# Loading and transposing K in column quarters with interleaved heads, in a one-token decode block

## The chip, the cores and the metric

The kernel runs on one core of one Trainium2 chip. The metric is the device time of one execution in microseconds; the time before is the median of three runs. A profile of one execution stands beside it, with its own span.

## What is computed

One token `x` of 1024 numbers goes through a layer norm, and then through an attention branch and an MLP branch whose results are added to it. Everything in memory is bf16. Cut to what matters:

```python
xn = layernorm(x)                                  # 1 x 1024
q  = xn @ wq                                       # 32 heads of 128
k, v = last 4096 rows of k_cache, v_cache          # 4 kv heads, 4096 x 128 each
o  = softmax(q . k / sqrt(128)) . v                # 8 query heads share one kv head
A  = o @ wo                                        # wo: 4096 x 1024
h  = gelu(layernorm(xn) @ w1 + b1)                 # w1: 1024 x 3584
B  = h @ w2 + b2                                   # w2: 3584 x 1024
out = x + A(xn) + B(xn)
```

In the code the residual `x` and the bias `b2` enter the final accumulator `accf` through a small matmul. K and V of the window are 4 MB each, wq and wo 8 MB each, w1 and w2 7 MB each: 39.85 MB are read once, and almost nothing is written.

## The kernel before, in words

The large operands go through a ring of four slots of 32 KB per partition (4 MB each). The tiles in the order of their requests are `k_sb`, `wq0`, `wq1`, `kt_scr` (a scratch tile that no DMA fills), `w10`, `w11`, `v_sb`, `w20`, `w21`, `wo0`, `wo1`. A tile's load is issued on SP's queue when the slot's last user has finished; SP takes its issues in the order of the program, so a load that waits holds up those behind it. Small loads (`x_sb`, `b1_row`, `xb2`) go on ACT's queue. The framework orders the instructions of each engine and adds the waits; a DMA also waits for the completion counter that it reuses (there are eight, handed out in turn).

**K.** Each of the four heads is loaded by one DMA of 1 MB (line 73). Partition p gets 32 consecutive keys of the head, 8 KB in one run. The scores need K with the head's 128 features on the partitions. That is done in two steps. DVE transposes each head in blocks of 32x32 into `kt_scr` (line 185, four instructions of 128x4096). Then 64 copies of 32x1024 put the blocks in their places in `kT`; they are shared out between ACT (line 199, 26 copies) and DVE (line 201, 38 copies). `kT` holds, for each head, 4096 keys side by side.

**q and the scores.** 64 matmuls (line 237) make q from `xnT` and the two halves of wq. q is copied to `q_sb`, transposed on PE (`qT_ps`, line 261) and spread into `qm` (line 266), which holds for each kv head its 8 query columns and zeros elsewhere. The scores of all 32 heads over a quarter R of the keys are then the sum of four matmuls, one per kv head (line 275), each with 512 keys as the moving operand; the four R write four groups of 32 partitions of the PSUM tile `sp`.

**Softmax and output.** Maximum over the row (lines 283 to 294), exponential on ACT (line 297), a block transpose (`eTb`, line 299), the row sums (`rs_ps`, line 301), and 32 matmuls with V into `o_all` (line 319), of which a mask keeps each head's own kv head (line 322).

**MLP and the end.** `acch` takes 64 matmuls with the halves of w1 (line 257: `w10`, then `w11`), then gelu (line 312) and a transpose to `hT` (line 314). The final product runs over 28+28 chunks of w2 and 16+16 chunks of wo (line 338 into `accf`; the last eight chunks on line 353 into `acct`, in four pieces of 256 columns). `wo1` is loaded in five DMAs that become smaller towards the end (line 228). The result is added up on DVE (line 356) and stored.

Of the kernel before, what the change touches and what calls it, by code (L numbers as in the profile page):

```python
# [9 lines left out]
BF16 = mybir.dt.bfloat16  # L10
# [6 lines left out]
def kernel(  # L17
# [14 lines left out]
    nc = tc.nc  # L32
    P = 128
    D = A_x.shape[-1]
    Hkv = A_k_cache.shape[1]
    Sk = A_k_cache.shape[2]
# [5 lines left out]
    W = min(4096, max(256, Sk // 4))  # L42
    C = D // P
    NCH = W // P
    NJQ = NQ // 512
    WQ4 = W // 4
# [7 lines left out]

    consts = ctx.enter_context(tc.tile_pool(name="consts", bufs=1))
    small = ctx.enter_context(tc.tile_pool(name="small", bufs=2))
    ring = ctx.enter_context(tc.tile_pool(name="ring", bufs=4))
    ps_acc = ctx.enter_context(tc.tile_pool(name="ps_acc", bufs=1, space=bass.MemoryType.PSUM))
    ps_tp = ctx.enter_context(tc.tile_pool(name="ps_tp", bufs=1, space=bass.MemoryType.PSUM))
    ps_f = ctx.enter_context(tc.tile_pool(name="ps_f", bufs=2, space=bass.MemoryType.PSUM))  # L60

    RING_ELEMS = 16384

    def ring_tile(name):
        return ring.tile([P, RING_ELEMS], BF16, tag="ring", name=name, align_bytes=256)

    x_flat = A_x.rearrange("a b d -> (a b d)")


    k_sb = ring_tile("k_sb")  # L70
    k4 = k_sb[:].rearrange("p (g c d) -> p g c d", g=Hkv, c=NCH)
    for g in range(Hkv):
        nc.sync.dma_start(out=k4[:, g, :, :], in_=A_k_cache[0, g, Sk - W:Sk, :].rearrange("(p c) d -> p c d", p=P))
    x_sb = consts.tile([P, C], BF16)
    nc.scalar.dma_start(out=x_sb[:], in_=x_flat.rearrange("(p c) -> p c", p=P))
    xb2 = consts.tile([34, 512], BF16)
# [10 lines left out]
    for i in range(2):  # L87
        t = ring_tile(f"wq{i}")
        tv = t[:].rearrange("p (r n) -> p r n", r=4)
        nc.sync.dma_start(out=tv, in_=wq_v[:, 4 * i:4 * i + 4, :])  # L90
        wq_tiles.append(tv)
    kt_scr = ring_tile("kt_scr")


# [13 lines left out]
    qm = consts.tile([P, Hkv, Hq], BF16)  # L108
# [69 lines left out]
                         start=True, stop=False, tile_position=(pr, pr))  # L178


    kT = consts.tile([P, Hkv, W], BF16)
    scr = kt_scr[:].rearrange("p (g f) -> p g f", g=Hkv)
    k2 = k_sb[:].rearrange("p (g f) -> p g f", g=Hkv)
    for g in range(Hkv):
        nc.vector.transpose(out=scr[:, g, :], in_=k2[:, g, :])  # L185
    nc.vector.tensor_reduce(out=sel4[:], in_=ident_f[:].rearrange("p (r h) -> p h r", r=4), axis=AX.X, op=ALU.add)
    act_share = [11, 8, 5, 2]
    act_moves, dve_moves = [], []
    for g in range(Hkv):
        T4 = scr[:, g, :].rearrange("p (c a j) -> p c a j", a=4, j=32)  # L190
        k = 0
        for R in range(4):
            for Cd in range(4):
                src = T4[32 * R:32 * R + 32, :, Cd, :]
                dst = kT[32 * Cd:32 * Cd + 32, g, WQ4 * R:WQ4 * (R + 1)].rearrange("p (c j) -> p c j", j=32)
                (act_moves if k < act_share[g] else dve_moves).append((dst, src))
                k += 1
    for (dst, src) in act_moves:
        nc.scalar.copy(out=dst, in_=src)  # L199
    for (dst, src) in dve_moves:  # L200
        nc.vector.tensor_copy(out=dst, in_=src)  # L201

    for i in range(2):
        t = ring_tile(f"w1{i}")
# [3 lines left out]
    v_sb = ring_tile("v_sb")  # L208
    v4 = v_sb[:].rearrange("p (g c d) -> p g c d", g=Hkv, c=NCH)
    for g0, g1 in ((0, 2), (2, 3), (3, 4)):  # L210
        src = A_v_cache[0, g0:g1, Sk - W:Sk, :].rearrange("g (p c) d -> p g c d", p=P)
# [20 lines left out]
    for i, w3 in enumerate(wq_tiles):  # L232
        for r in range(4):
            c = 4 * i + r
            for j in range(NJQ):
                b, t = divmod(j, 4)
# [10 lines left out]
    for j in range(8):  # L247
        t, b = divmod(j, 2)
        nc.tensor.matmul(acch[32 * t:32 * t + 1, b, :NH], lhsT=ones_bf[0:1, 0:1], rhs=b1_row[:, j * NH:(j + 1) * NH],
                         start=True, stop=False, tile_position=(0, 32 * t))  # L250
    for i, w3 in enumerate(w1_tiles):
        for r in range(4):
            c = 4 * i + r
            for b in range(2):
                for t in range(4):
                    j = 2 * t + b
# [5 lines left out]
    for g in range(Hkv):  # L262
        b, th = divmod(g, 2)
        src = qT_ps[:, b * 4:(b + 1) * 4, 64 * th:64 * th + 64:32]
        dst = qm[:, g, g * REP:(g + 1) * REP].rearrange("p (t hh) -> p hh t", t=2)
# [4 lines left out]
    for a in range(WQ4 // 512):  # L270
        sp = ps_f.tile([P, 512], FP32, tag="pf", name="sp")
        for R in range(4):
            for g in range(Hkv):
                c0 = WQ4 * R + 512 * a
                nc.tensor.matmul(sp[32 * R:32 * R + 32, :], lhsT=qm[:, g, :], rhs=kT[:, g, c0:c0 + 512],  # L275
                                 start=(g == 0), stop=(g == Hkv - 1), tile_position=(0, 32 * R))
        if a % 2 == 0:
            nc.vector.tensor_copy(out=sc[:, a * 512:(a + 1) * 512], in_=sp[:])
        else:
            nc.scalar.copy(out=sc[:, a * 512:(a + 1) * 512], in_=sp[:])  # L280
# [63 lines left out]
    for t in range(4):  # L344
        half, w = divmod(t, 2)
        src = accf[32 * half:32 * half + 1, 256 * w:256 * w + 256]
# [41 lines left out]
```

## Time and profile before

| what | value |
|---|---|
| median of 3 runs | 102.22 us (102.2 to 102.45) |
| span of the profiled execution | 100.7 us |
| read from memory over the span | 39.86 MB, mean 396 GB/s |
| busy: PE, DVE, ACT, POOL | 49.1, 49.4, 34.2, 4.5 us |
| DVE, block transposes (line 185) | 4 of 4.41 us |
| DVE, kT copies (line 201) | 38 of 0.419 us |
| ACT, kT copies (line 199) | 26 of 1.042 us |
| PE, scores (line 275) | 32 matmuls, 3.8 us together |

The span is what the profiler recorded of one execution; the timed runs lie about 1.5 us above it, and the profiled execution has no time of its own beside its span. Busy time of an engine is a sum over the whole span; the page's second part cuts the span into 40 slices of 2.52 us and gives, for each engine, the busy share of each slice in tenths. The "DMA" row is the mean share of the sixteen DMA engines, and GB/s what they moved. The chain that ended last is followed back from the last instruction, at each step to what released it. The trace also records each DMA packet with its size, start and duration, which the text calls the packet records.

### The profile page before, as it was taken

The page shows a single profiled execution, that of the slowest core. Times are in us where ns is not written, and L with a number is a line of the kernel's source. Part 1 is how long each engine was busy: PE and PEld are TensorE (multiplying, and loading weights), DVE is VectorE, ACT ScalarE, POOL GpSimd, SP SyncE. Part 2 cuts the span into 40 slices and gives each one's busy share as a digit, 9 for nine tenths or more (in the row PEclk, how much of TensorE's full clock was granted, in tenths as well). Part 3 has the DMA queues.
Part 4 walks back from the last instruction along what each step waited for, and adds up shares of the span by engine and source line. Part 5 has one row for each costly group of instructions (what it writes and reads, how often), then busy time and mean ns, then how long its engine had stood idle before and what let it go on. Part 6 is the DMA issues. An engine that isn't in the chain of part 4 may idle for free.

```text
span 100.7 us, 962 instructions
## 1 busy us (share of the span) xinstructions
PE 49.1 (49%) x361; PEld 19.2 (19%) x361; DVE 49.4 (49%) x91; ACT 34.2 (34%) x37; POOL 4.5 (4%) x18
## 2 busy tenths in 40 slices
PE   0027200008500930482882935999389930299830
PEld 0012200003100300121531222334133410023310
DVE  4335499999999999997126115510630000000130
ACT  0500002999999999962001045400000000000110
POOL 7105300000000000000000000000000000000000
PEclk9999999999985579555555555569976997559995
DMA  3899999999999998999999998999999998999910
GB/s 52 346 434 436 482 443 482 443 430 417 417 417 391 456 444 376 459 444 382 391 423 430 436 511 387 467 428 433 433 410 413 456 456 384 423 420 408 369 33 1
DMA packets 3031, 39.92 MB, mean 396 GB/s; under 512 B 458, under 2 KB 466, under 8 KB 851
## 3 DMA queue, kind: packets, MB, share of 16 engines
q1 hardware_dynamic: 2872, 39.85, 93.3%
q8 instruction: 3, 0.05, 0.2%
q10 hardware_dynamic: 154, 0.01, 0.1%
q14 instruction: 2, 0.01, 0.0%
HBM read 39.86 MB, written 0.00 MB: 396 GB/s over the span
## 4 chain that ended last, share of the span: by engine, by line
DVE 37%; DMA 24%; PE 19%; issue 9%; POOL 3%; ACT 2%; SPq 2%; POOLq 1%; DVEq 0%; ACTq 0%
DMA wo<-in_A_wo_dram 24%; DVE kt_scr L185 17%; DVE kT L201 16%; PE o_all L319 10%; PE sp L275 4%; PE acch L257 3%; SPq L228 2%; ACT e L297 1%; DVE eTb L299 1%; DVE m_loc L283 1%; PE qT_ps L261 1%; DVE q_sb L240 1%; POOLq L383 1%; ACT sc L280 1%; POOL spread L113 1%
## 5 line engine op out<-in xcount | busy, mean ns | idle before, releaser
L199 ACT COPY kT<-kt_scr 32x1024 bf16<-32x1024 bf16 x26 | 27.1, 1042 | 12.9 <-DVE kt_scr L185 12.6
L185 DVE STREAM_TRANSPOSE kt_scr<-k_sb 128x4096 bf16<-128x4096 bf16 x4 | 17.4, 4412 | 0.0
L201 DVE COPY kT<-kt_scr 32x1024 bf16<-32x1024 bf16 x38 | 15.9, 419 | 0.5
L237 PE MATMUL accq<-wq,xnT 128*1 128x512 bf16 x64 | 7.1, 622 | 17.9 <-DMA wq<-in_A_wq_dram 17.9
L350 ACT COPY bulk<-accf 1x256 f32<-1x256 f32 x2 | 0.7, 361 | 31.7 <-DVE bulk L348 31.7
L348 DVE COPY bulk<-accf 1x256 f32<-1x256 f32 x2 | 0.8, 416 | 21.3 <-PE accf L338 20.8
L319 PE MATMUL o_all<-v_sb,eTb 128*32 128x512 bf16 x32 | 9.9, 485 | 1.0 <-DVE zcol L310 1.0
L338 PE MATMUL accf<-wo,o 128*1 128x512 bf16 x48 | 7.1, 465 | 6.1 <-DMA wo<-in_A_wo_dram 6.1
L257 PE MATMUL acch<-w,yT 128*1 128x448 bf16 x64 | 6.3, 574 | 5.6 <-DMA w<-in_B_w_dram 5.6
L338 PE MATMUL accf<-w,hT 128*1 128x512 bf16 x56 | 7.9, 452 | 0.0
L237 PEld LDWEIGHTS <-xnT 128*1 128x1 bf16 x64 | 2.1, 115 | 22.1 <-issue 22.1
L319 PEld LDWEIGHTS <-eTb 128*32 128x32 bf16 x32 | 3.7, 119 | 6.8 <-issue 3.8
L338 PEld LDWEIGHTS <-o 128*1 128x1 bf16 x48 | 2.4, 98 | 10.8 <-issue 8.9
L275 PE MATMUL sp<-kT,qm 128*32 128x512 bf16 x32 | 3.8, 629 | 0.3 <-DVE qm L266 0.3
L257 PEld LDWEIGHTS <-yT 128*1 128x1 bf16 x64 | 2.0, 116 | 9.4 <-issue 9.4
L131 PE MATMUL ln_tot<-st,ones_f 128*128 128x1 f32 x2 | 0.6, 362 | 6.4 <-DVE st L129 6.4
L338 PEld LDWEIGHTS <-hT 128*1 128x1 bf16 x56 | 2.7, 96 | 4.7 <-issue 2.3
L322 DVE TENSOR_TENSOR o_m<-o_all,grs 32x512 f32<-32x512 f32 x1 | 0.7, 679 | 5.6 <-PE o_all L319 5.6
L297 ACT ACTIVATE e<-sc,nmx 128x1024 bf16<-128x1024 f32 x1 | 1.1, 1147 | 5.7 <-DVE nmx L294 5.7
L314 DVE STREAM_TRANSPOSE hT<-h_sb 128x896 bf16<-128x896 bf16 x1 | 1.7, 1711 | 2.4 <-ACT h_sb L312 2.4
L261 PE MATMUL qT_ps<-ident,q_sb 128*128 128x128 bf16 x8 | 1.2, 308 | 2.3 <-DVE q_sb L240 2.3
L275 PEld LDWEIGHTS <-qm 128*32 128x32 bf16 x32 | 2.1, 133 | 1.4 <-issue 0.9
(84 smaller groups left out, 34.4 us busy)
## 6 DMA issues: line engine op xcount, KB each, us to landing
w<-in_B_w_dram SPq DMA_DIRECT2D x4, 3584.0 KB, 26.1
wq<-in_A_wq_dram SPq DMA_DIRECT2D x2, 4096.0 KB, 21.6
k_sb<-in_A_k_cache_dram SPq DMA_DIRECT2D x4, 1024.0 KB, 7.1
wo<-in_A_wo_dram SPq DMA_DIRECT2D x1, 4096.0 KB, 29.4
v_sb<-in_A_v_cache_dram SPq DMA_DIRECT2D x1, 2048.0 KB
v_sb<-in_A_v_cache_dram SPq DMA_DIRECT2D x2, 1024.0 KB, 23.4
wo<-in_A_wo_dram SPq DMA_DIRECT2D x1, 2048.0 KB
wo<-in_A_wo_dram SPq DMA_DIRECT2D x1, 1024.0 KB, 23.1
```

The source lines that it names most:

```text
L185: nc.vector.transpose(out=scr[:, g, :], in_=k2[:, g, :])
L199: nc.scalar.copy(out=dst, in_=src)
L201: nc.vector.tensor_copy(out=dst, in_=src)
L228: nc.sync.dma_start(out=tv[:, a:b, :], in_=wo_v[:, nr * i + a:nr * i + b, :])
L237: nc.tensor.matmul(accq[32 * t:32 * t + 1, b, :], lhsT=xnT[:, c:c + 1], rhs=w3[:, r, j * 512:(j + 1) * 512], start=(c == 0), stop=(c == C ...
L257: nc.tensor.matmul(acch[32 * t:32 * t + 1, b, :NH], lhsT=yT[:, c:c + 1], rhs=w3[:, r, j * NH:(j + 1) * NH], start=False, stop=(c == C - 1) ...
L261: nc.tensor.transpose(qT_ps[:, b * 4 + hh, :], q_sb[:, b, hh * Dh:(hh + 1) * Dh], ident[:])
L275: nc.tensor.matmul(sp[32 * R:32 * R + 32, :], lhsT=qm[:, g, :], rhs=kT[:, g, c0:c0 + 512], start=(g == 0), stop=(g == Hkv - 1), tile_posit ...
L297: nc.scalar.activation(out=e128[:], in_=sc[:], func=ACT.Exp, bias=nmx[:], scale=scale, accum_out=l_loc[:])
L314: nc.vector.transpose(out=hT[:], in_=h_sb[:].rearrange("p (d c) -> p c d", c=CW2))
L319: nc.tensor.matmul(o_all[:].rearrange("h g d -> h (g d)"), lhsT=eTb[:, 32 * c:32 * c + 32], rhs=v4[:, :, c, :], start=(c == 0), stop=(c == ...
L338: nc.tensor.matmul(accf[32 * half:32 * half + 1, :], lhsT=vec[kind](c), rhs=wap[:, half * 512:(half + 1) * 512], start=False, stop=(idx == ...
```

## The change

K is loaded by two DMAs instead of four. Partition p = 4r+g now holds head g's 128 consecutive keys from row 128r on, 32 KB in one run; the first DMA brings the first 8 KB of every partition (1 MB), the second the remaining 24 KB (3 MB). The four block transposes work on column quarters s of the tile, 32 keys of each partition, instead of heads, so the first needs the first DMA alone. `kT` is laid out as [R][s][1024], where the heads alternate from column to column. ACT copies six of the sixteen block pairs quarter by quarter (24 copies of 32x1024), DVE the other ten for all quarters at once (10 copies of 32x4096). The score matmuls pick a head's keys out of `kT` with a stride of four elements and write their columns of `sp` in an order with a stride of four, so that `sp` has the keys in the same order as before.

The ring's four slots are now named by hand. In the built program the last users differ in one place: w20 follows `kt_scr` and w21 follows `w10`, where it was the other way round. The built program also changes the order on two engines. On DVE the first block transpose stands in the first layer norm, between `ve` (line 143 before) and `xn_f` (line 146 before); the other three stand behind `yT` as before. On PE the transposes of q and the scores stand ahead of both halves of w1, the first half of w1 follows behind `mT_ps`, and the second half behind `rs_ps`, ahead of `o_all`. SP's first wq load no longer waits for a completion counter.

```diff
-    ring = ctx.enter_context(tc.tile_pool(name="ring", bufs=4))
+    ring = ctx.enter_context(tc.tile_pool(name="ring", bufs=1))
...
+    slots = {"k_sb": 0, "wq0": 1, "wq1": 2, "kt_scr": 3, "w10": 1, "w11": 0, "v_sb": 2, "w20": 3, "w21": 1, "wo0": 0, "wo1": 2}
+
     def ring_tile(name):
-        return ring.tile([P, RING_ELEMS], BF16, tag="ring", name=name, align_bytes=256)
+        return ring.tile([P, RING_ELEMS], BF16, tag=f"ring{slots[name]}", name=name, align_bytes=256)
...
-    k4 = k_sb[:].rearrange("p (g c d) -> p g c d", g=Hkv, c=NCH)
-    for g in range(Hkv):
-        nc.sync.dma_start(out=k4[:, g, :, :], in_=A_k_cache[0, g, Sk - W:Sk, :].rearrange("(p c) d -> p c d", p=P))
+    k_v = A_k_cache[0, :, Sk - W:Sk, :].rearrange("g (r c) d -> r g (c d)", r=P // Hkv)
+    for a, b in ((0, W), (W, 4 * W)):
+        nc.sync.dma_start(out=k_sb[:, a:b], in_=k_v[:, :, a:b])
...
-    kT = consts.tile([P, Hkv, W], BF16)
-    scr = kt_scr[:].rearrange("p (g f) -> p g f", g=Hkv)
-    k2 = k_sb[:].rearrange("p (g f) -> p g f", g=Hkv)
-    for g in range(Hkv):
-        nc.vector.transpose(out=scr[:, g, :], in_=k2[:, g, :])
+    NS = 4
+    kT = consts.tile([P, 4, NS, W // NS], BF16)
+    scr = kt_scr[:].rearrange("p (s f) -> p s f", s=NS)
+    k2 = k_sb[:].rearrange("p (s f) -> p s f", s=NS)
+    for s in range(NS):
+        nc.vector.transpose(out=scr[:, s, :], in_=k2[:, s, :])
...
-    act_share = [11, 8, 5, 2]
-    act_moves, dve_moves = [], []
-    for g in range(Hkv):
-        T4 = scr[:, g, :].rearrange("p (c a j) -> p c a j", a=4, j=32)
...
-    for (dst, src) in act_moves:
-        nc.scalar.copy(out=dst, in_=src)
-    for (dst, src) in dve_moves:
-        nc.vector.tensor_copy(out=dst, in_=src)
+    T5 = kt_scr[:].rearrange("p (s c a j) -> p s c a j", s=NS, a=4, j=32)
+    pairs = [(R, Cd) for R in range(4) for Cd in range(4)]
+    ACT_PAIRS = 6
+    for s in range(NS):
+        for (R, Cd) in pairs[:ACT_PAIRS]:
+            nc.scalar.copy(out=kT[32 * Cd:32 * Cd + 32, R, s, :].rearrange("p (c j) -> p c j", j=32),
+                           in_=T5[32 * R:32 * R + 32, s, :, Cd, :])
+    for (R, Cd) in pairs[ACT_PAIRS:]:
+        nc.vector.tensor_copy(out=kT[32 * Cd:32 * Cd + 32, R, :, :].rearrange("p s (c j) -> p (s c) j", j=32),
+                              in_=kt_scr[32 * R:32 * R + 32, :].rearrange("p (c a j) -> p c a j", a=4, j=32)[:, :, Cd, :])
...
-                c0 = WQ4 * R + 512 * a
-                nc.tensor.matmul(sp[32 * R:32 * R + 32, :], lhsT=qm[:, g, :], rhs=kT[:, g, c0:c0 + 512],
+                kv = kT[:, R, :, :].rearrange("p u (b r h) -> p h b u r", r=8, h=Hkv)[:, g, 16 * a:16 * a + 16]
+                nc.tensor.matmul(sp[32 * R:32 * R + 32, :].rearrange("p (b r u) -> p b u r", r=8, u=4), lhsT=qm[:, g, :], rhs=kv,
                                  start=(g == 0), stop=(g == Hkv - 1), tile_position=(0, 32 * R))
```

More of the change, by code (lines that the diff above doesn't have):

```diff
@@ L178 @@
                          start=True, stop=False, tile_position=(pr, pr))
-    kT = consts.tile([P, Hkv, W], BF16)
-    scr = kt_scr[:].rearrange("p (g f) -> p g f", g=Hkv)
-    k2 = k_sb[:].rearrange("p (g f) -> p g f", g=Hkv)
-    for g in range(Hkv):
-        nc.vector.transpose(out=scr[:, g, :], in_=k2[:, g, :])
-    nc.vector.tensor_reduce(out=sel4[:], in_=ident_f[:].rearrange("p (r h) -> p h r", r=4), axis=AX.X, op=ALU.add)
-    act_share = [11, 8, 5, 2]
-    act_moves, dve_moves = [], []
-    for g in range(Hkv):
-        T4 = scr[:, g, :].rearrange("p (c a j) -> p c a j", a=4, j=32)
[L191 to L197, printed above, removed]
-    for (dst, src) in act_moves:
-        nc.scalar.copy(out=dst, in_=src)
-    for (dst, src) in dve_moves:
-        nc.vector.tensor_copy(out=dst, in_=src)
+    NS = 4
[4 more added lines that the diff above has]
+        nc.vector.transpose(out=scr[:, s, :], in_=k2[:, s, :])
+    nc.vector.tensor_reduce(out=sel4[:], in_=ident_f[:].rearrange("p (r h) -> p h r", r=4), axis=AX.X, op=ALU.add)
+    T5 = kt_scr[:].rearrange("p (s c a j) -> p s c a j", s=NS, a=4, j=32)
[8 more added lines that the diff above has]
+                              in_=kt_scr[32 * R:32 * R + 32, :].rearrange("p (c a j) -> p c a j", a=4, j=32)[:, :, Cd, :])
     for i in range(2):
```

## Prediction

> **What bounds the kernel now.** I read the page's forty slices first, because the shares of whole engines (DVE 49%, PE 49%) say little about a kernel in stages.
>
> ```profile
> span 100.7 us, 962 instructions
> ...
> DVE  4335499999999999997126115510630000000130
> ACT  0500002999999999962001045400000000000110
> ...
> DMA  3899999999999998999999998999999998999910
> ...
> q1 hardware_dynamic: 2872, 39.85, 93.3%
> ```
>
> DVE and ACT are full from about 13 to 47 us: that is the transposing of K, the work this change rewrites. But the DMA row is full from the second slice to the end. The table by stretches sharpens it (columns: us, PE, PEld, DVE, ACT, POOL busy, granted clock, DMA share, GB/s):
>
> ```profile
> 13.00:31.00 18.00, 3.52 (x32) 1.06 (x32) 17.94 (x7) 13.77 (x14) 0.00 (x0) 0.96 1.01 435
> 32.00:50.00 18.00, 9.14 (x84) 3.64 (x87) 15.10 (x39) 12.93 (x13) 0.00 (x0) 0.59 0.99 420
> 61.00:76.00 15.00, 12.47 (x50) 4.78 (x52) 4.78 (x10) 2.44 (x3) 0.00 (x0) 0.73 1.00 431
> 95.00:96.00 1.00, 0.49 (x16) 0.26 (x9) 0.52 (x2) 0.36 (x1) 0.00 (x0) 1.00 0.62 225
> 96.00:97.00 1.00, 0.66 (x12) 0.27 (x12) 0.01 (x1) 0.36 (x1) 0.00 (x0) 1.00 0.11 43
> ```
>
> At a DMA share of 1.0 all sixteen DMA engines are busy; between 3 and 95 us the stream never falls dry. In the last microsecond before 97 a share of 0.11 means 1.8 of 16 engines: a straggler ends the load. Now the chain that ended last (start us, us, what):
>
> ```profile
> 71.39 0.02 issue
> 71.40 0.33 SPq L228
> ...
> 73.20 24.12 DMA wo<-in_A_wo_dram
> 97.32 0.04 issue
> 97.36 0.31 PE acct L353 x4
> ```
>
> The chain runs through the transposes and copies because the last pieces of wo were issued when o_all released the slot of v_sb. It overstates that link. The 24.12 us are no transfer of 256 KB: at 430 GB/s they are 10 MB, w2, wo0 and wo1 queued in front. wo0 ended at 86.4 by the packet records, so the issue at 71.4 came about 15 us before the queue would have run dry. So the kernel is one 39.85 MB stream, from the first packet at 2.1 to the last at 97.3 us, and a tail of 3.4 us.
>
> **Part by part.**
>
> *Two K loads instead of four.* K is 4 MB in 512 packets of 8 KB; it becomes 128 of 8 KB and 128 of 24 KB. The packet records give 309 ns for 8 KB and 1213 for 32 KB, so a packet costs (4x309-1213)/3 = 7.7 ns beyond its bytes. Each engine carries 16 packets fewer: 16x7.7 = 0.12 us less, and two completions fewer at 9 ns each. Sum: -0.14 us, on the path, because the stream is the path.
>
> *Interleaved heads.* Consecutive packets of an engine now lie 16 MB apart instead of 8 KB. The nearest row is the first load of v_sb, whose packets alternate between two heads 16 MB apart: its packets take 309 ns, and v_sb as a whole ran at 424 GB/s. So I take zero. The lower bound is zero too, as 309 ns is already the per-byte pace of 32 KB packets. For the upper end see the first rival.
>
> The Trainium skill (DMA: Bandwidth & Descriptors, Latency and other measured facts) warns that HBM row pitches at large powers of two cut the copy rate to about half from 4 MiB up. If that held for this pattern, the K stage would double, by an estimate from that page; the v_sb row contradicts it here.
>
> *Small loads and issues.* On SP two K issues of about 0.4 us go, and wq no longer waits for x_sb (3.1 us today): its two issues move from 5.95 to about 2. K is still in transfer until 12, so nothing is gained. But x_sb, b1 and xb2 on ACT's queue alternate packet by packet with K. Their last packet started at 7.95; against 0.91 us packets I expect about 12 (seven rounds more at 0.91). x_sb itself lands some 0.7 us later.
>
> *First transpose ahead of the layer norm's end.* It now stands between `ve` and `xn_f` on DVE. Queued behind it for 4.41 us are xn_f, xnT and yT; the PE waits for them. xnT moves from 10.2 to about 15, needed at 22.9, when wq0 lands: covered by 8 us. yT goes to about 17, needed after 41. Start of transposes two to four: 12.6+4.4+0.4 (x_sb) = 17.4; end 17.4+3x4.41 = 30.6, against 30.03 today. w11 waits for that; its slot is needed when w10 has landed, at 41.7. Hidden by 11 us; without that cover it would cost 0.6.
>
> *Copies.* DVE: 38 of 32x1024 at 419 ns (15.9 us) become 10 of 32x4096. Bounds: four times 419 = 1.68 us each, or, taking 150 ns of 419 as fixed (the 157 ns of the 8-element copy L266), 0.16+4x0.26 = 1.20 us. I take the second, since L266 shows the fixed part: 12 us, end at 42.7 (upper bound 47.4; today 46.47). ACT: 24 instead of 26 at 1.04 us, six per quarter, ends at about 41. Nothing of it reaches the stream: w20, which now takes kt_scr's slot first, issues at 43 to 48, and v_sb keeps the queue busy until 60.2.
>
> *Order on PE.* qT and the scores move in front of both halves of w1, and the second half moves behind rs_ps. So the end of `sp` is 42.7+0.7 (q_sb)+1.25 (qT)+0.4 (qm)+3.8 = 48.9. The chain behind it to rs_ps took 7.8 us (52.6 to 60.4); then w11's 3.2 us stand in front of o_all: 59.9. v_sb lands at 60.2 and takes over as the late one. o_all: 9.9 us, until about 70.2 (today 71.4). w21 waits for w10's matmuls, at 54.5; w20 lands near 69. All covered.
>
> *Strided scores.* The 32 matmuls L275 read bf16 at 8-byte steps and write PSUM at 16-byte steps. No row shows a strided matmul. Below: no cost (3.8 us as now; less is excluded, as the columns are the same). Above: no overlap at all between the four column groups, 32x629 ns = 20.1 us, +16.3. Nearest strided row: DVE's reduction L324, 1007 ns for 512 strided elements against 679 for L322, 1.5 times. I take 1.5, +1.9 us, inside the cover of 10 us (second rival).
>
> The Trainium skill (Advanced Engine Details and Errata, PSUM Cachelines) states that any non-contiguous PSUM pattern slows matmuls significantly, without a figure; by it the score stage is where this change loses, by my working it does not matter below 3.6 times.
>
> **The sum**, against the profiled span of 100.7 us: -0.14, giving 100.55. The runs' median of 102.22 lies 1.5 us above the span, outside the recorded program; so 102.1. I forecast 102.05, leaving a little for the straggler.
>
> **The rivals.**
>
> *The K load slows down.* Each engine's share of K is now cut out of a 32-row source with four heads, and onto which partitions each engine writes at one moment is not shown by any row. If engines get in each other's way, the cost is undiluted. Price: a dozen packets of w1 between 34.5 and 38 us were stretched from 1062 to 1127-1305 ns; about 1220, 15%, on K's 9.9 us is +1.5. Two engines sharing one path, 309 to 618 ns, is +9.9, 112. It decides from 3% on (0.3 us). Against it: v_sb's row. For it: that row has 128 rows on both sides. 102.4 to 112; chance 0.14.
>
> *The scores become the bound.* PE must start on wo by 90.3 (97.3 less 5.2 for 48 matmuls at full clock and 1.8 to 2 for the last 32), so o_all must end by about 80: 10 us later than forecast. That is sp at 13.8 us, 3.6 times today's. At the upper bound of 20.1 us the end moves by about 16.3-10 = +6, 108. Chance 0.08.
>
> *The straggler catches up.* Most engines finish at 95.5 to 96, one at 97.3. It lost its time in packets stretched from 1062 to about 1550 ns at 47.1 and 68.8, beside 16 KB instruction fetches, and at the start. If fewer instructions or other small-load times spare it one such hit, the end comes 0.5 to 1.0 us earlier: 101.2 to 101.7. For it: 28 DVE instructions fewer. Against: PE, with most instructions, keeps its 720. Chance 0.18.
>
> *DMA-bound, nothing visible moves*: 102.05, own range 101.75 to 102.4. Chance 0.60.
>
> **How the numbers follow.** This kernel's measurement can tell about 0.3% (0.3 us) from no change, so "same" is 101.9 to 102.5. Of the 0.60, 0.45 fall inside, 0.13 below, since -0.14 is half of the bound, and 0.02 above. The straggler's 0.18 is faster. The two slow rivals give 0.22, of which 0.02 inside the bound. Faster 0.31, same 0.47, slower 0.22. The range leaves out 0.05 below 101.4 and 0.15 above 103.6: it takes in the 15% of the first rival, but not its doubling nor most of the second.
>
> **What would show it.** Right: the DMA row full from the second slice to 95 us, K's second load landed near 12, transposes ending near 31, kT copies 1.2 us each, sp under 10 us, o_all starting when v_sb has landed, the last chain again ending in wo. Wrong: a GB/s row under 400 in slices 2 to 5 (first rival); PE accf on wo no longer waiting for DMA, 6.1 us today (second); the last wo landing before 97.0 with the same bytes (third). A dry stretch anywhere between 13 and 95 us would refute my covers.

## The result, and the profile after

The changed kernel takes 102.73 us (median of 11 runs, 102.45 to 102.92) beside 102.27 for the kernel before (11 runs): ratio 1.0034, 95% interval 1.0019 to 1.0048. By this ratio it is slower by about 0.35 us (0.19 to 0.49; the two medians lie 0.46 apart), where the forecast was 102.05, a gain of 0.17. The sign was wrong. The fewer packets that the forecast built on are there all the same, but a late start of about 0.45 us that it left out outweighs them.

The page of the changed kernel, its first two parts and the third:

```profile
span 100.7 us, 929 instructions
...
DVE  4659779999999997102706320000900000000040
ACT  0500797899999972002044500000000000000020
...
DMA  1899999999999898998999998998999999999910
...
q1 hardware_dynamic: 2584, 39.85, 92.8%
```

DVE is done with K in the sixteenth slice (39 us) instead of the nineteenth, ACT in the fifteenth instead of the eighteenth, and 288 DMA packets are gone. Neither moved the end. In the DMA row the first digit is 1 instead of 3; behind it three slices show an 8 for a 9 and one a 9 for an 8. The span itself can't show the loss: this execution took 102.45 us, the lowest of its eleven, whose spans go from 100.7 to 101.1. So the loss has to be looked for where each execution is alike, at the start. SP's issues (start us, us for all of the group), first of the kernel before, then of the changed one:

```profile
0.80 2.02 SPq L73 DMA_DIRECT2D k_sb<-in_A_k_cache_dram  x4
5.95 0.81 SPq L90 DMA_DIRECT2D wq<-in_A_wq_dram  x2
```

```profile
0.80 1.29 SPq L75 DMA_DIRECT2D k_sb<-in_A_k_cache_dram  x2
2.13 1.43 SPq L92 DMA_DIRECT2D wq<-in_A_wq_dram  x2
```

Four issues took 2.02 us and two take 1.29. Taken singly, the first one went from 378 to 654 ns. Now the first microseconds by stretches (the last two columns are the DMA share and GB/s), before and after:

```profile
1.00:2.00 1.00, 0.00 (x0) 0.00 (x0) 0.79 (x4) 0.00 (x0) 0.95 (x5) 1.00 0.82 98
3.00:4.00 1.00, 0.00 (x0) 0.00 (x0) 0.28 (x1) 1.00 (x1) 0.00 (x0) 1.00 0.99 410
```

```profile
1.00:2.00 1.00, 0.00 (x0) 0.00 (x0) 0.79 (x4) 0.00 (x0) 0.95 (x5) 1.00 0.04 1
3.00:4.00 1.00, 0.41 (x2) 0.41 (x2) 0.51 (x3) 0.88 (x1) 0.00 (x0) 1.00 0.88 352
```

Before, DMA engines were at work on K by 2 us; after, the stretch from 1 to 2 us holds nothing but x_sb's first small packets. By the packet records, set on a clock on which SP's first issue starts at 0.80, K's first packet starts at 1.82 us before and at 2.27 after. (The 2.1 us of the prediction was read with the records 0.3 us late; differences are not touched by that.) From there the K stage is as fast as it was: its 4.19 MB take 11.00 us before (to 12.82) and 10.93 after (to 13.20). So the stream starts 0.45 us late, and the K stage does not make it up.

These two profiles do not show the loss at the end. When w1's first packet starts, the changed kernel is 0.40 us behind (32.10 against 31.70), but the last packet of wo ends at 96.92 against 96.99. Packets were stretched more in the execution before: the durations of its packets of 1 KB and more add up to 0.96 us per engine above the undisturbed ones, against 0.61 after. That a late start reaches the end is shown by the times of the runs, here and below.

The changed kernel's chain ends in wo, as before:

```profile
37.52 23.14 DMA v_sb<-in_A_v_cache_dram
60.66 0.14 issue
60.80 9.68 PE o_all L317 x32
70.48 0.02 issue
...
72.29 24.90 DMA wo<-in_A_wo_dram
97.19 0.04 issue
97.24 0.31 PE acct L351 x4
```

Now the chain goes from load to load; the transposes are no longer in it, and o_all starts when v_sb has landed.

### The profile page after: what moved, and what is told of

Same layout as the page of the kernel before. It is cut to its first block, busy times and chain, and to the rows that moved or that the text cites. A ratio compares the mean times of both kernels' runs of the same rounds, so it can differ in the third digit from the quotient of the medians.

```text
span 100.7 us, 929 instructions
## 1 busy us (share of the span) xinstructions
PE 48.8 (48%) x361; PEld 18.9 (19%) x361; DVE 45.0 (45%) x63; ACT 32.1 (32%) x35; POOL 4.5 (4%) x18
## 4 chain that ended last, share of the span: by engine, by line
DMA 78%; PE 13%; SPq 4%; issue 1%; DVE 0%; DVEq 0%
DMA wq<-in_A_wq_dram 30%; DMA wo<-in_A_wo_dram 25%; DMA v_sb<-in_A_v_cache_dram 23%; PE o_all L317 10%; PE accq L235 4%; SPq L226 2%; SPq L75 1%; SPq L210 1%; SPq L92 1%; DVE res L354 0%; PE acct L351 0%; DVEq L354 0%
## 5 line engine op out<-in xcount | busy, mean ns | idle before, releaser
L195 ACT COPY kT<-kt_scr 32x1024 bf16<-32x1024 bf16 x24 | 25.0, 1043 | 7.4 <-DVE kt_scr L188 7.1
L198 DVE COPY kT<-kt_scr 32x4096 bf16<-32x4096 bf16 x10 | 12.2, 1219 | 0.2
L336 PE MATMUL accf<-wo,o 128*1 128x512 bf16 x48 | 8.2, 522 | 6.5 <-DMA wo<-in_A_wo_dram 6.5
L273 PE MATMUL sp<-kT,qm 128*32 128x512 bf16 x32 | 5.9, 922 | 0.3 <-DVE qm L264 0.3
L255 PE MATMUL acch<-w,yT 128*1 128x448 bf16 x64 | 3.4, 352 | 0.0
L278 ACT COPY sc<-sp 128x512 f32<-128x512 f32 x1 | 0.6, 585 | 6.9 <-PE sp L273 6.9
L276 DVE COPY sc<-sp 128x512 f32<-128x512 f32 x1 | 0.7, 691 | 3.8 <-PE sp L273 3.8
```

The lines of the kernel that those rows point to most:

```text
L195: nc.scalar.copy(out=kT[32 * Cd:32 * Cd + 32, R, s, :].rearrange("p (c j) -> p c j", j=32), in_=T5[32 * R:32 * R + 32, s, :, Cd, :])
L198: nc.vector.tensor_copy(out=kT[32 * Cd:32 * Cd + 32, R, :, :].rearrange("p s (c j) -> p (s c) j", j=32), in_=kt_scr[32 * R:32 * R + 32, :] ...
L255: nc.tensor.matmul(acch[32 * t:32 * t + 1, b, :NH], lhsT=yT[:, c:c + 1], rhs=w3[:, r, j * NH:(j + 1) * NH], start=False, stop=(c == C - 1) ...
L273: nc.tensor.matmul(sp[32 * R:32 * R + 32, :].rearrange("p (b r u) -> p b u r", r=8, u=4), lhsT=qm[:, g, :], rhs=kv, start=(g == 0), stop=( ...
L336: nc.tensor.matmul(accf[32 * half:32 * half + 1, :], lhsT=vec[kind](c), rhs=wap[:, half * 512:(half + 1) * 512], start=False, stop=(idx == ...
```

## The experiments

Theory 1: the end of the kernel is the end of the stream, the stream starts 0.45 us later because the first issue on SP takes longer, and that goes through one for one; 0.14 comes back through fewer packets. Theory 2: the 24 KB packets or the 16 MB steps cost time somewhere later in the stream. Theory 3: the strided scores or the new order on PE reach the end.

**A plain source.** Same cuts, same partitions, same number of DMAs:

```diff
-    k_v = A_k_cache[0, :, Sk - W:Sk, :].rearrange("g (r c) d -> r g (c d)", r=P // Hkv)
+    k_v = A_k_cache[0, 0, Sk - 4 * W:Sk, :].rearrange("(p c) d -> p (c d)", p=P)
```

> The changed kernel with the same two K loads (8 and 24 KB per partition, all 128 partitions), but from one contiguous 4 MB piece of one head, so that the source has two dimensions (128 rows) instead of three (32 rows, 4 heads, a run). It leaves out the right keys: the scores are of other rows. Theory 1 (late start: SP's first K issue takes 654 instead of 378 ns, the first K packet starts at 2.27 instead of 1.82 us, and the whole stream with it): first issue about 0.4 us, first packet about 1.8, time 102.27-0.14, about 102.1 to 102.25, some 0.45 below the changed kernel's 102.73. Theory 2 (the packets of 24 KB or the loss of two DMAs make a later part of the stream slower): first issue as short as before, time stays near 102.7. Theory 3 (strided scores or the new order on PE reach the end): time stays near 102.7.

Measured: 102.34 us beside 102.39, ratio 0.9995 (0.9982 to 1.0007). SP's K issues, and the stretch from 1 to 2 us:

```profile
0.80 0.85 SPq L75 DMA_DIRECT2D k_sb<-in_A_k_cache_dram  x2
```

```profile
1.00:2.00 1.00, 0.00 (x0) 0.00 (x0) 0.79 (x4) 0.00 (x0) 0.95 (x5) 1.00 0.48 74
```

The first issue is back at 378 ns, the first packet at 1.80, and the loss is gone, with the transposes by quarters, the strided scores and PE's new order all in place. This excludes theory 3 and the size of the packets. It removes the late start and the 16 MB steps together, so the two still had to be told apart.

**The new loads alone**, in the kernel before:

```diff
-    for g in range(Hkv):
-        nc.sync.dma_start(out=k4[:, g, :, :], in_=A_k_cache[0, g, Sk - W:Sk, :].rearrange("(p c) d -> p c d", p=P))
+    k_v = A_k_cache[0, :, Sk - W:Sk, :].rearrange("g (r c) d -> r g (c d)", r=P // Hkv)
+    for a, b in ((0, W), (W, 4 * W)):
+        nc.sync.dma_start(out=k_sb[:, a:b], in_=k_v[:, :, a:b])
```

> The kernel before with nothing changed but K's loads: the two interleaved loads of the change into k_sb, with the old transposes, copies and scores. The heads are mixed in k_sb, so the scores are of mixed keys. Theory 1: the whole loss comes with the loads: first packet about 2.27, time 102.27+0.45-0.14, about 102.6 to 102.75. Theory 3: no loss, 102.1 to 102.3. Theory 2: 102.7, but with a first packet that does not explain it.

Measured: 102.71, ratio 1.0027 (1.0017 to 1.0038); first issue 649 ns, first packet 2.23. SP's K issues:

```profile
0.80 1.29 SPq L74 DMA_DIRECT2D k_sb<-in_A_k_cache_dram  x2
```

The loads alone bring the loss with them, within the intervals.

**The start delayed by other means.** The kernel before, with x_sb's load moved from ACT's queue to SP's, ahead of the K loads:

```diff
-    nc.scalar.dma_start(out=x_sb[:], in_=x_flat.rearrange("(p c) -> p c", p=P))
+    nc.sync.dma_start(out=x_sb[:], in_=x_flat.rearrange("(p c) -> p c", p=P))
```

> The kernel before, with x_sb's small load issued on SP ahead of the four K loads instead of on ACT: the same bytes, K's first issue one issue later. Theory 1: the first K packet starts some 0.4 to 0.5 us later than 1.82, and that goes through to the end one for one: about 102.7, ratio 1.003 to 1.005. If the start of the stream were caught up later: ratio 1.000.

Measured: 102.72 beside 102.30, ratio 1.0042 (1.0026 to 1.0059); K's first packet at 2.31. SP's issues:

```profile
0.81 0.39 SPq L73 DMA_DIRECT2D x_sb<-in_A_x_dram  x1
1.26 2.21 SPq L75 DMA_DIRECT2D k_sb<-in_A_k_cache_dram  x4
```

K has its old four plain loads here, heads apart, 8 KB packets. A start later by 0.49 us alone costs 0.43 us (0.27 to 0.60): the pass-through is one for one within the interval.

**The slow issue hidden.** The changed kernel with the first half of wq loaded ahead of K, nothing left out; `load_wq(i)` holds the body of the old loop, and the two K loads and the small loads stand between its calls:

```diff
+    load_wq(0)
     k_sb = ring_tile("k_sb")
...
-    for i in range(2):
-        t = ring_tile(f"wq{i}")
-        tv = t[:].rearrange("p (r n) -> p r n", r=4)
-        nc.sync.dma_start(out=tv, in_=wq_v[:, 4 * i:4 * i + 4, :])
-        wq_tiles.append(tv)
+    load_wq(1)
```

> The changed kernel with the first half of wq loaded ahead of K: the stream's first DMA then has a plain source, and the two slow K issues (0.65 and 0.58 us) lie behind 9.7 us of wq0. Nothing is left out. Theory 1: first issue about 0.4 us, first packet of the stream at about 1.8 to 1.9 us, time 102.73-0.45 = about 102.3 or a little less (0.998 to 1.000 of the kernel before), although K lands some 10 us later; the later transposes stay covered (o_all ends at about 76, needed by 80). If the loss lay in the 16 MB steps between an engine's packets or in the 24 KB packets, wherever they stand in the stream: no gain, 102.7.

Measured: 102.32 beside 102.30, ratio 1.0002 (0.9987 to 1.0016). SP's first issues:

```profile
0.80 0.38 SPq L79 DMA_DIRECT2D wq<-in_A_wq_dram  x1
1.24 1.45 SPq L86 DMA_DIRECT2D k_sb<-in_A_k_cache_dram  x2
```

The stretch from 1 to 2 us (DMA share and GB/s last), and o_all's piece of the chain:

```profile
1.00:2.00 1.00, 0.00 (x0) 0.00 (x0) 0.79 (x4) 0.00 (x0) 0.95 (x5) 1.00 1.17 328
```

```profile
64.27 7.09 PE o_all L321 x32
```

The interleaved loads are unchanged, and their issues are even a little slower (635 and 768 ns), but they lie behind 4 MB of wq0; the stream starts at 1.81, and the loss is gone. So neither the 16 MB steps between the heads of neighbouring partitions nor the 24 KB packets cost anything that can be measured: theory 2 falls. The transposes now end 10 us later and o_all starts at 64.27 instead of 60.80, with no loss: this is the cover that the prediction worked with. This version repairs the changed kernel; it doesn't beat the kernel before.

**Plain scores.** The changed kernel with

```diff
-                kv = kT[:, R, :, :].rearrange("p u (b r h) -> p h b u r", r=8, h=Hkv)[:, g, 16 * a:16 * a + 16]
-                nc.tensor.matmul(sp[32 * R:32 * R + 32, :].rearrange("p (b r u) -> p b u r", r=8, u=4), lhsT=qm[:, g, :], rhs=kv,
+                kv = kT[:, R, g, 512 * a:512 * a + 512]
+                nc.tensor.matmul(sp[32 * R:32 * R + 32, :], lhsT=qm[:, g, :], rhs=kv,
```

> The changed kernel with the 32 score matmuls reading 512 neighbouring columns of kT and writing sp without a stride, which mixes heads and keys. Theory 1: sp falls from 5.9 to about 3 to 3.8 us, the score chain ends earlier, o_all still starts when v_sb has landed (60.7), time unchanged at 102.6 to 102.8. Theory 3: time falls by 0.3 to 0.5, to about 102.3.

Measured: 102.72, ratio 1.0033 (1.0022 to 1.0045), as slow as the changed kernel. The score groups, of the changed kernel and then of this one (mean ns of one behind the busy time), both at a granted clock of 1.00:

```profile
L273 PE MATMUL sp<-kT,qm 128*32 128x512 bf16 x32 | 5.9, 922 | 0.3 <-DVE qm L264 0.3
```

```profile
L273 PE MATMUL sp<-kT,qm 128*32 128x512 bf16 x32 | 3.8, 630 | 0.4 <-DVE qm L264 0.4
```

The stride costs 2.1 us in its own stage and nothing at the end.

**Small loads behind K.** Is the issue slow because ACT issues x_sb at the same moment? In the changed kernel all four small loads went to SP, between the two K loads (`nc.sync.dma_start` in place of `nc.scalar.dma_start`):

```diff
+    nc.sync.dma_start(out=k_sb[:, 0:W], in_=k_v[:, :, 0:W])
...
+    nc.sync.dma_start(out=k_sb[:, W:4 * W], in_=k_v[:, :, W:4 * W])
```

> The changed kernel, but the four small loads (x, b1, b2) are issued on SP between the first and the second K load, so that nothing on ACT's queue competes with the first K issue. If the late first packet comes from x_sb's descriptors being made ahead of K's (x_sb's packets now start at 1.81, K's at 2.27): first issue about 0.4, first K packet about 1.8, time 102.1 to 102.3. If it comes from the three-dimensional source itself: first issue stays near 0.65, first packet near 2.1 to 2.3, time about 102.7. Theories 2 and 3: 102.7 whatever the first packet does.

Measured: 103.07, ratio 1.0061 (1.0045 to 1.0077). SP's first issue:

```profile
0.79 0.67 SPq L74 DMA_DIRECT2D k_sb<-in_A_k_cache_dram  x1
```

With nothing on ACT's queue, the first issue takes 665 ns and K's first packet starts at 2.29. So x_sb is not in the way; that its packets come first (at 1.81) is a consequence. The further 0.3 us of this version arise in the K stage, while the small loads and the second K load go through one queue: that load's first packet starts at 5.55 instead of 5.39, and K's 4.19 MB end at 13.52 instead of 13.20. What exactly stretches them was not followed.

**Which shape makes the issue slow.** Two versions with two heads instead of four, each run once, with the wrong keys: source and destination both of 128 rows by 2 heads (half runs, 4 and 12 KB), and a source of 64 rows by 2 heads against 128 partitions (8 and 24 KB, as in the change). In the cut below the first added line is that of the one version, the second that of the other; the first version also splits the destination by head.

```diff
-    k_v = A_k_cache[0, :, Sk - W:Sk, :].rearrange("g (r c) d -> r g (c d)", r=P // Hkv)
+    k_v = A_k_cache[0, 0:2, Sk - 2 * W:Sk, :].rearrange("g (p c) d -> p g (c d)", p=P)
+    k_v = A_k_cache[0, 0:2, Sk - 2 * W:Sk, :].rearrange("g (r c) d -> r g (c d)", r=P // 2)
```

> The changed kernel with K's two loads from two heads, 128 rows first on both sides (128 x 2 x 2048 and 128 x 2 x 6144 elements, in the manner of the v_sb load); wrong keys, 4 and 12 KB packets. One look at SP's first issue and the first packet. If three dimensions as such make the issue long: about 0.65 us and 2.25. If it is the unequal split (32 rows of source against 128 partitions): about 0.39, as v_sb's first load, and 1.8 to 1.9.

> The changed kernel with K's two loads from two heads, source 64 rows x 2 heads against 128 partitions, runs of 8 and 24 KB as in the change; wrong keys. One look at SP's first issue and the first packet. If the unequal split makes the issue long: about 0.6 us and about 2.25. If four heads are needed for it: about 0.4 and 1.85.

| first load: source rows against 128 partitions | first issue, ns | first packet, us |
|---|---|---|
| 128, before | 378 | 1.82 |
| 128, plain source | 378 | 1.80 |
| 128, wq0 first | 377 | 1.81 |
| 128 x 2 heads | 449 | 1.95 |
| 64 x 2 heads | 658 | 2.28 |
| 32 x 4 heads, changed kernel | 654 | 2.27 |
| 32 x 4 heads, in the kernel before | 649 | 2.23 |
| 32 x 4 heads, plain scores | 651 | 2.24 |
| 32 x 4 heads, nothing on ACT's queue | 665 | 2.29 |

Here a third dimension costs the first issue some 70 ns, though this load also has 256 packets instead of 128; a source whose outer rows don't match the partitions costs about 275 with 128 packets as before, and two heads are enough for it. The packets start some 0.45 us later, more than the issue itself is longer; what fills the rest can't be seen in the trace. The 64 x 2 version took 102.85 in its one run. The 128 x 2 version took 103.57: its K stage lasted 12.36 us instead of 10.93, and its 4 KB packets took 243 ns on average at the start (median 166), where the 4 KB packets of wo take 159 at the end. What stretched them was not followed.

## Why the prediction was wrong

**The step that failed** is "Small loads and issues": "On SP two K issues of about 0.4 us go [...] K is still in transfer until 12, so nothing is gained." It counted the issues and hid them behind the transfer. That holds for every issue but the first, which has no transfer in front of it, and the first was priced at 0.4 us by the rows of a plainer shape; it took 0.654, and the wait from its end to K's first packet grew by another 0.17, for which the prediction had no term. The sum that should have stood there, by what the runs showed, is +0.45 (first packet) - 0.14 (packets) = +0.31, 102.6. Measured: +0.35 (0.19 to 0.49). The runs show that this late start turned the sign; why such a source makes the issue and the wait longer stays open.

**The packet term** of -0.14 holds in the packet records (24 KB packets take 912 ns where 0.91 us was worked out; the undisturbed durations sum to 92.72 us per engine instead of 92.85). In time it is below what the runs can tell: -0.05 us (-0.18 to +0.07) with the plain source.

**The base of the sum.** Runs whose span is on record lie 1.7 to 1.9 us above it, not 1.5, so the profiled execution before, with 100.7, stands for about 102.4 and not for the median. Adding 1.5 brought the forecast back to the median, so its gain of 0.17 is not touched. Its 86.4 for the end of wo0 is early: wo0's last packet ended at 87.14 on the clock used here, which makes the margin of 15 us larger.

**The first rival** named the thing, a 32-row source against 128 partitions, but set its price in the packets' pace, where it costs nothing; it costs in the issue.

**Small loads.** x_sb was expected 0.7 us later and came 2.8 earlier (xf at 3.19 instead of 5.95), since its packets now start ahead of K's. The last small packets, expected four us later, came two later (9.56 instead of 7.65). yT was expected at about 17 and came at 13.4. The reason was the same unseen order at the start.

**Covered work** was right, with sizes close where rows existed. DVE's copies were expected at 1.20 us each; their group on the page of the changed kernel:

```profile
L198 DVE COPY kT<-kt_scr 32x4096 bf16<-32x4096 bf16 x10 | 12.2, 1219 | 0.2
```

Transposes ended at 26.7 and the copies at 39.0 (expected 30.6 and 42.7, mostly through the misjudged x_sb). The strided scores were taken at 1.5 times, from two DVE rows of different operations; 5.9 against 3.8 is 1.5 times. With such a source for it, that agreement is luck. The Trainium skill's warning on non-contiguous PSUM patterns (Advanced Engine Details and Errata, PSUM Cachelines) is borne out in direction by this row, though the runs change the read and the write stride together. Its warning on row pitches at large powers of two (DMA: Bandwidth & Descriptors, Latency and other measured facts), measured there for copies between HBM tensors, does not show in these loads: with 16 MB between neighbouring partitions' heads, 24 KB took 912 ns.

**The second rival** did not occur: among the waits of the changed kernel PE still waits for wo, 6.5 us in total.

```profile
PE accf L336 <- DMA wo<-in_A_wo_dram: 6.5, 1, 6.5
```

**The third rival** did not occur either. The straggler is still there (DMA share 0.13 from 96 to 97 us), and the three instruction fetches of 16 KB on queue 8 as well, although DVE has 28 instructions fewer.

## What to carry to other kernels

In a kernel whose DMA engines are full from the first packet to the last, time is the start of the first packet plus bytes over rate plus the tail; a saving in any engine in between is worth nothing, and a delay of the first packet is worth all of itself: here 2.1 us of score time were worth nothing, and 0.49 us of delay cost 0.43. So give the first issue of such a stream the plainest shape, source rows matching the 128 partitions, and put the loads with interleaved or regrouped sources behind it. Price an issue by the row of its own shape and place, not by the mean of issues on its queue.

## What the runs showed of the hardware

SP's first issue took 377 to 378 ns for 128 rows on both sides, whether 1 MB of K or 4 MB of wq (391 for x_sb's 2 KB); 449 with two heads as a further dimension on both sides (388 for v_sb's first load of that form, in mid-kernel); and 649 to 665 where 32x4 or 64x2 rows meet 128 partitions. The delay until the first packet grew by more than the issue did, 0.45 us against 0.28. Shape is not all that sets the time: issues of the plain shape that came later took from 327 ns (w21 in the changed kernel, alone at 51.2 us) to 657 (the fourth of K's issues before) and 789 (the second of wq in the changed kernel). So an issue is compared with one at the same place.

Of two queues that issue at the same time, the one with the shorter issue had its first packet first in the kernels before and after. SP and ACT both issued at 0.80; ACT's issue of x_sb took, before and after,

```profile
0.80 0.41 ACTq L75 DMA_DIRECT2D x_sb<-in_A_x_dram  x1
```

```profile
0.80 0.39 ACTq L77 DMA_DIRECT2D x_sb<-in_A_x_dram  x1
```

Before, SP's first issue was the shorter (378 ns), and x_sb's first packet followed K's (2.38 after 1.82); after, it was the longer (654), and x_sb's led (1.81 before 2.27). It is no rule: with x_sb issued on SP ahead of K, ACT's first issue, b1's of a single 7 KB packet, took 520 ns against 391, and its packet still came first (1.70 against 1.80).

The 32 plain score matmuls took 3.8 us both at a granted clock of 0.50 (kernel before, 48.8 to 52.6 us) and at 1.00 (plain scores, 41.4 to 45.2 us), while single matmuls of 128x448 with w1 took 581 ns at 0.50 before and 352 at 1.00 after. What bounds the plain scores was not followed.
